# An interleaved attention and mixer kernel on one core: other planner constants, three mixer weight slots, later output projections

## The chip, the cores and the metric

The kernel runs on one NeuronCore of one Trainium2 chip. The metric is the device time of one execution in microseconds (us). Several runs of the same program are taken and the median is quoted. The profile is one further execution, recorded by the hardware profiler.

## What is computed

Four layers follow each other on a sequence of 2048 tokens of width 640: attention, mixer, attention, mixer (the same weights twice).

```
x = x + A(layernorm(x));  x = x + B(layernorm(x));  x = x + A(layernorm(x));  x = x + B(layernorm(x))
A: for each segment s of 32 tokens:  h = concat(mem, x_s)            # 8 + 32 rows
     q, k, v = h@Wq, h@Wk, h@Wv      # 32 heads of 192
     p = softmax(mask(q k^T * scale));  o = (p v) @ Wo;  mem = o[:8];  output o[8:]
B: h = gelu(layernorm(x)@w1); shift four column groups of h by +1, -1, +2, -2 tokens
   x1 = x + shifted(h)@w2;  out = x1 + gelu(layernorm(x1)@w3)@w4      # w3: 640 x 1536
```

The attention is a recurrence: segment s+1 needs the first 8 output rows of segment s. So a segment's output projection must be finished before the next segment's projections begin.

## The kernel before, in words

**Steps and lanes.** The attention runs in 69 steps (`T_A`). In a step lane 0 handles segment t of the first attention layer and lane 1 segment t-5 of the second one, side by side as 80 columns (2 x 40). The first five steps and the last five have one lane, 40 columns. A step works through 8 groups of 4 heads, two groups to a pair (`proj_pair`, `attend`, lines 479 to 629). For a pair, k, q and v are projected (line 495: 30 matmuls for a group and kind, each with its own 128x128 weight load). Then come, for each group, the scores `pss` (L559), mask and row minimum on VectorE (L570), exp on ScalarE (L577), the row sums on VectorE (L581 to L583), the transposed weights `pst` (L591), their copy `PT` (L596), `pso` (L605), its copy `oT` (L611) and the output projection into `psy` (L622, 30 matmuls against the resident `wo`). At the step's end ScalarE copies the memory rows of `psy` into the next step's `hT` (L640) and VectorE the others into `yTB` (L652); the next step's first matmul waits for `hT`.

**Mixer.** Every two steps one chunk of 64 tokens of both lanes (128 rows) goes through the mixer (`chunk`, `chunk_end`): psx, psl (transposes back), layernorm, w1 into `psh` (L873), gelu, w2 into `hs` (L901), layernorm, w3 into `psh2` in two halves (L933), gelu (L703 to L717), w4 into `y2` (L956, named y in the profile), the stores (L974) and the next attention's input. These instructions stand between those of the attention.

**Weights.** Part of Wk, Wq, Wv and all of Wo stay in SBUF. The rest is loaded again in every step: per pair 3 loads for k, 3 for q and 2 for v, 384 KB each (L420, tile `wst`), into a ring of 7 slots (`RING_A`). The mixer's weights are loaded again for each chunk, into a ring of 2 slots (`RING_B`, L443 to L449, tile `wstB`): w1 and w2 in three pieces (2, 2 and 1 rows of 128), w3 in 2 x 3, w4 in 6. All these loads are issued by SyncE's queue, in one order. A load waits there until the last matmul that reads its slot is done, and what is queued behind it waits too.

**The order of the work** is set before the launch by a planner (`Plan`, lines 66 to 217). Each operation has an engine, a duration, a due time and the buffers that it reads and writes. The planner simulates the engines and always places the operation that can start first, and among those that start at nearly the same time the one due earliest. What it places is then written out in that order on each engine. Its constants: `LAT` and `PE_LAT` are the handover from one engine to another, `DMA_RATE`, `DMA_LAT` and 0.8 us model a load (0.8 us, then the bytes at 380 GB/s one load after another, then 1.2 us).

**Homes.** PSUM has 8 banks: one for `psy` (class "y"), five for the attention's other tiles (class "A"), two for the mixer (class "B"). `oT` has 5 buffers. `xres` (bf16) holds the mixer's residual input, `xw` (f32) the sum, `gl` (f32) the gelu's intermediate, `PT` has two buffers.

Of the kernel before, what the change touches and what calls it, by code (L numbers as in the profile page):

```python
# [61 lines left out]
class Op:  # L62
    __slots__ = ("e", "d", "due", "fn", "n", "succ", "ready", "slots", "start", "end", "dma", "i")


class Plan:
# [8 lines left out]
    def add(self, e, d, due, fn, r=(), w=(), a=(), dma=0, queue=None):  # L75
        op = Op()
        op.e, op.d, op.due, op.fn, op.dma = e, d, due, fn, dma
# [34 lines left out]
    def place(self):  # L112
# [40 lines left out]
        while left:  # L153
# [67 lines left out]
def kernel(  # L221
# [107 lines left out]
    sm = [ctile([P, 16], f32, f"sm{i}") for i in range(4)]  # L329
# [15 lines left out]
    st4 = [ctile([P, 24], f32, f"st{i}") for i in range(4)]  # L345
# [11 lines left out]
    ALIAS = {("vx",): ("vb",), ("xo",): ("vb",), ("vx2",): ("uw",)}  # L357
# [26 lines left out]
    def mm_us(n, m=128, k=1):  # L384
        return k * (max(min(64, m), n) / 2400.0 + 0.0025)
# [44 lines left out]
    def load_b(nm, a, e, due, half=0):  # L430

        b = Slotted("rb", None)
        b.make = lambda: wring.tile([P, SLOT], bf16, name="wstB", tag=f"rb{b.slot}")
        n = e - a
        W = GW if nm == "w3" else Dm
# [4 lines left out]
        def fn(op):  # L440
            v = view()
            if nm == "w1":
                nc.sync.dma_start(out=v, in_=w1_v[:, a:e, :])  # L443
            elif nm == "w3":
                nc.sync.dma_start(out=v, in_=w3_v[:, a:e, GW * half:GW * (half + 1)])
# [4 lines left out]
        add("SP", DMA_ISSUE, due - LEAD_B, fn, w=(b,), dma=P * n * W * 2, queue="wb")  # L450
# [14 lines left out]
    def attention_step(t):  # L465
# [9 lines left out]
        psy = ps("y", [P, KC, NS], f32, "psy")  # L475
# [3 lines left out]
        def proj_pair(pr):  # L479
            s0 = base + sl * 2 * pr  # L480
            for kind, off in (("k", 0.0), ("q", 0.2), ("v", 0.5)):
                wbs, wv = load_pair(kind, pr, s0 + off * 2 * sl, LEAD_A)
                for j in range(2):
# [37 lines left out]
                    else:  # L521
# [12 lines left out]
                        for hf in range(2):  # L534
                            def fe(op, pvt=pvt, V_=V_, hf=hf):
                                src = T(pvt)[0:N, GWH * hf:GWH * (hf + 1)].rearrange("n (a b) -> n a b", a=2)
                                if hf:
                                    nc.vector.tensor_copy(out=v_runs(V_, hf)[0:N], in_=src)  # L538
                                else:
                                    nc.scalar.copy(out=v_runs(V_, hf)[0:N], in_=src)  # L540
# [3 lines left out]
        def v_runs(V_, hf):  # L544

            return V_[:, 512 * hf:512 * hf + 640].rearrange("n (a b) -> n a b", a=2)[:, :, 0:Dh]

        def attend(g):
# [31 lines left out]
            def f3(op):  # L580
                nc.vector.tensor_reduce(out=sm_[0:N, 4:4 + HG], in_=Pb[0:N, :, 0:N], axis=AX.X, op=ALU.add)  # L581
                nc.vector.reciprocal(out=sm_[0:N, 8:8 + HG], in_=sm_[0:N, 4:4 + HG])
                nc.vector.tensor_tensor(out=Pb[0:N, :, 0:N], in0=Pb[0:N, :, 0:N],  # L583
                                        in1=sm_[0:N, 8:8 + HG].unsqueeze(2).to_broadcast([N, HG, N]), op=ALU.mult)
# [8 lines left out]
            Pt = PT[G % 2]  # L593
# [3 lines left out]
            add("ACT", act_us(HG * N), hi - 4, f5, r=(pst,), w=(B("PT", G % 2),))  # L597
            pso = ps("A", [P, GC, NS], f32, "pso")

            def f6(op):  # L600
                o = T(pso)
                for hf in range(2):
                    for i2, col, c, st, sp in ((0, 0, 0, True, True), (0, 128, 1, True, False), (1, 256, 1, False, True),
                                               (1, 384, 2, True, True)):
                        nc.tensor.matmul(out=o[:, 3 * hf + c, 0:N], lhsT=V_[0:N, 512 * hf + col:512 * hf + col + P],  # L605
                                         rhs=Pt[0:N, 2 * hf + i2, 0:N], start=st, stop=sp)
            add("PE", mm_us(N, k=8), hi - 3, f6, r=(B("PT", G % 2), B("V", G % 2, 0), B("V", G % 2, 1)), w=(pso,))
# [118 lines left out]
    def chunk_loads(c):  # L726
# [22 lines left out]
        if edge:  # L749
            def fz(op):  # L750
                nc.gpsimd.memset(xres[:], 0.0)
                nc.gpsimd.memset(lnx[0:4, :], 0.0)
            add("POOL", 1.0, base, fz, w=(B("xres"), B("lnx", "l")))
        for lane, a, b, w0 in todo:
# [4 lines left out]
        for lane, k0 in look:  # L759
# [5 lines left out]
        if s < NSEG:  # L765
# [8 lines left out]
    def chunk(c):  # L774
# [65 lines left out]
        if c + 1 < NCH:  # L840
            chunk_loads(c + 1)
# [81 lines left out]
        for half in range(2):  # L923
            pz2 = [ps("B", [P, 3, XB], f32, "psh2") for _ in range(2)]
            for i, (a, e) in enumerate(((0, 2), (2, 4), (4, KC))):
                due = D(0.75 + 0.3 * half + 0.05 * i)
                wb, wv = load_b("w3", a, e, due, half)

                def fw(op, a=a, e=e, wv=wv, pz2=pz2):
                    w = wv()  # L930
                    for kc in range(a, e):
                        for n in range(6):
# [3 lines left out]
                add("PE", mm_us(128, k=6 * (e - a)), due, fw, r=(wb, vTk), a=tuple(pz2))  # L936
            for i in range(2):
# [134 lines left out]
```

## Time and profile before

| | us |
|---|---|
| median of 3 runs (lowest, highest) | 3990.78 (3970.34, 3994.87) |
| the profiled execution: its time, its span | 3971.5, 3969.8 |
| TensorE busy (share of the span) | 3493.2 (88%) |
| VectorE, ScalarE, GpSimd busy | 2608.1 (66%), 1550.0 (39%), 257.6 (6%) |
| DMA moved, mean rate | 1107.57 MB, 279 GB/s |
| the 59 steps with two lanes (292 to 3622) | 3330 |

The span goes from the first to the last instruction. Busy time is the sum of an engine's instructions; the ends of matmuls are modelled, so a run of n matmuls shows a little more than n times the pace of one. "Idle before" and the waits name the instruction or transfer that came last before an engine went on. PE is TensorE, DVE VectorE, ACT ScalarE, POOL GpSimd, SP SyncE. The names in the profile leave out buffer numbers, so psv is both the attention's v and a mixer tile.

### The profile page before, as it was taken

To read this page: it belongs to the slowest core of one execution; us is meant where nothing else is said; L and a number is where in the kernel's file an instruction comes from. 1 tells how busy PE (TensorE), PEld (TensorE's weight loads), DVE (VectorE), ACT (ScalarE), POOL (GpSimd) and SP (SyncE) were. 2 spreads that over 40 slices of the span, in tenths; PEclk is the share of its full clock that TensorE was granted. 3 is DMA by queue.
4 is the path that set the end of the run, shared out by engine and by line. 5 is a ranking of instruction groups with operands and counts; after the bars stand their busy time and mean duration, and the time that the engine had idled before them with its cause. 6 is when DMAs were issued, how large, how long until landed. Compare 5 with 4: busy or idle time off the path is not lost.

```text
span 3969.8 us, 187915 instructions
## 1 busy us (share of the span) xinstructions
PE 3493.2 (88%) x84703; PEld 3320.3 (84%) x84703; DVE 2608.1 (66%) x7611; ACT 1550.0 (39%) x3516; POOL 257.6 (6%) x467
## 2 busy tenths in 40 slices
PE   6888999999898988899998998898989999889884
PEld 5878888888888888888888888888888888888772
DVE  2566666667676666676666666676666676766562
ACT  1334434444343444344444444444344444433331
POOL 0000000000000000000000000000000000000000
PEclk6999999999999999999999999999999999999995
DMA  9888777888787888788888888788878888778883
GB/s 367 290 309 292 268 273 273 292 276 281 270 301 271 275 279 283 268 276 281 287 281 277 285 276 290 262 280 277 276 272 282 281 297 274 271 271 313 312 281 90
DMA packets 489637, 1107.57 MB, mean 279 GB/s; under 512 B 50302, under 2 KB 200076, under 8 KB 488832
## 3 DMA queue, kind: packets, MB, share of 16 engines
q1 hardware_dynamic: 481600, 1082.42, 79.1%
q8 instruction: 662, 10.85, 1.1%
q0 software_dynamic: 7232, 13.13, 1.0%
q14 instruction: 143, 1.17, 0.1%
HBM read 1090.10 MB, written 5.24 MB: 276 GB/s over the span
## 4 chain that ended last, share of the span: by engine, by line
PE 59%; DMA 34%; issue 2%; ACT 2%; DVE 2%; SPq 0%; POOL 0%; POOLq 0%; ACTq 0%; DVEq 0%
DMA wstB<-in_B_w_dram 21%; PE psy L622 12%; PE psk L495 11%; PE psv L495 10%; PE psq L495 8%; DMA wst<-in_A_Wq_dram 7%; PE pvt L532 3%; DMA wst<-in_A_Wk_dram 3%; PE pss L559 3%; PE y L956 3%; PE pso L605 3%; PE psh L933 2%; PE pst L591 2%; DMA wst<-in_A_Wv_dram 1%; PE hs L901 1%
## 5 line engine op out<-in xcount | busy, mean ns | idle before, releaser
L495 PEld LDWEIGHTS <-wst 128*128 128x128 bf16 x26496 | 1076.6, 100 | 94.8 <-DMA wst<-in_A_Wq_dram 37.9
L622 PE MATMUL psy<-oT,wo 128*128 128x80 bf16 (+1 forms) x16560 | 713.5, 201 | 34.1 <-issue 14.2
L622 PEld LDWEIGHTS <-wo 128*128 128x128 bf16 x16560 | 647.2, 101 | 51.9 <-issue 31.7
L505 ACT CAST qT<-psq 128x480 bf16<-128x480 f32 (+1 forms) x552 | 291.8, 530 | 921.6 <-PE psq L495 921.1
L570 DVE CUSTOM_DVE_ANT_1 pss<-pss,mask 80x320 f32<-80x320 f32 (+1 forms) x512 | 246.0, 480 | 487.0 <-PE pss L559 429.3
L495 PE MATMUL psq<-hT,wst 128*128 128x80 bf16 (+1 forms) x9936 | 472.0, 200 | 35.2 <-DMA wst<-in_A_Wq_dram 30.3
L495 PE MATMUL psk<-hT,wst 128*128 128x80 bf16 (+1 forms) x9936 | 468.4, 199 | 27.6 <-DMA wst<-in_A_Wk_dram 22.2
L611 DVE CAST oT<-pso 128x480 bf16<-128x480 f32 (+1 forms) x552 | 341.9, 619 | 183.9 <-PE pso L605 179.7
L495 PE MATMUL psv<-hT,wv 128*128 128x80 bf16 (+1 forms) x9936 | 442.9, 201 | 11.2 <-DMA wv<-in_A_Wv_dram 6.6
L525 ACT CAST vF<-psv 128x480 bf16<-128x480 f32 (+1 forms) x552 | 291.4, 528 | 286.5 <-PE psv L495 281.3
L495 PEld LDWEIGHTS <-wv 128*128 128x128 bf16 x9936 | 391.7, 101 | 12.9 <-DMA wv<-in_A_Wv_dram 7.3
L540 ACT COPY V<-pvt 80x384 bf16<-80x384 bf16 (+1 forms) x552 | 262.4, 475 | 304.3 <-PE pvt L532 255.7
L495 PE MATMUL psk<-hT,wk 128*128 128x80 bf16 (+1 forms) x6624 | 320.6, 199 | 45.8 <-ACT hT L640 40.0
L495 PE MATMUL psv<-hT,wst 128*128 128x80 bf16 (+1 forms) x6624 | 352.1, 201 | 7.0 <-DMA wst<-in_A_Wv_dram 6.2
L538 DVE COPY V<-pvt 80x384 bf16<-80x384 bf16 (+1 forms) x552 | 190.2, 349 | 242.9 <-ACT V L540 163.0
L519 DVE CAST kT<-psk 64x160 bf16<-64x160 f32 (+1 forms) x1104 | 336.8, 305 | 8.2
L577 ACT ACTIVATE Pm<-pss,sm 80x320 bf16<-80x320 f32 (+1 forms) x552 | 278.4, 505 | 141.4 <-DVE sm L570 138.9
L495 PE MATMUL psq<-hT,wq 128*128 128x80 bf16 (+1 forms) x6624 | 320.3, 199 | 3.7 <-DMA wq<-in_A_Wq_dram 3.3
L513 DVE CAST kT<-psk 128x320 bf16<-128x320 f32 (+1 forms) x552 | 255.4, 463 | 93.6 <-PE psk L495 83.8
L495 PEld LDWEIGHTS <-wk 128*128 128x128 bf16 x6624 | 270.4, 100 | 54.1 <-issue 53.5
L532 PE MATMUL pvt<-ident,vF 128*80 128x128 bf16 (+1 forms) x3312 | 286.7, 224 | 2.7 <-issue 1.2
L596 ACT COPY PT<-pst 80x320 bf16<-80x320 bf16 (+1 forms) x552 | 222.5, 403 | 170.0 <-PE pst L591 167.6
(108 smaller groups left out, 4603.0 us busy)
## 6 DMA issues: line engine op xcount, KB each, us to landing
wst<-in_A_Wk_dram SPq DMA_DIRECT2D x828, 384.0 KB, 5.1
wst<-in_A_Wq_dram SPq DMA_DIRECT2D x828, 384.0 KB, 5.9
wst<-in_A_Wv_dram SPq DMA_DIRECT2D x552, 384.0 KB, 4.8
wstB<-in_B_w_dram SPq DMA_DIRECT2D x350, 320.0 KB, 5.4
wstB<-in_B_w_dram SPq DMA_DIRECT2D x140, 384.0 KB, 5.5
wstB<-in_B_w_dram SPq DMA_DIRECT2D x70, 192.0 KB, 5.2
wstB<-in_B_w_dram SPq DMA_DIRECT2D x70, 160.0 KB, 4.5
wo<-in_A_Wo_dram SPq DMA_DIRECT2D x8, 960.0 KB, 12.3
```

The source lines that it names most:

```text
L495: nc.tensor.matmul(out=o[:, cc, 0:N], lhsT=wv(kc, GW * j + cc * P, GW * j + (cc + 1) * P), rhs=h[:, kc, c0:c0 + N], start=(kc == 0 and cc ...
L505: nc.scalar.copy(out=q[:, :, 0:N], in_=T(pq)[:, :, 0:N])
L513: nc.vector.tensor_copy(out=k4[:, :, 0::3, 0:N], in_=p4[:, :, 0::2, 0:N])
L519: nc.vector.tensor_copy(out=k4[r0:r1, :, jj, 0:N], in_=p4[r0:r1, :, 1, 0:N])
L525: nc.scalar.copy(out=vf[:, :, 0:N], in_=T(pq)[:, :, 0:N])
L532: nc.tensor.transpose(out=o[0:N, c * P:(c + 1) * P], in_=vf[:, c, 0:N], identity=ident[:, :])
L540: nc.scalar.copy(out=v_runs(V_, hf)[0:N], in_=src)
L570: nc.vector.tensor_tensor_reduce(out=o, in0=o, in1=maskt.unsqueeze(1).to_broadcast([N, HG, N]), scale=-scale, scalar=3.0e38, op0=ALU.add, ...
L577: nc.scalar.activation(out=Pb[0:N, :, 0:N], in_=o, func=ACT.Exp, bias=sm_[0:N, 0:1], scale=-1.0)
L596: nc.scalar.copy(out=Pt[0:N, :, 0:N], in_=T(pst)[0:N, :, 0:N])
L611: nc.vector.tensor_copy(out=o_[:, :, 0:N], in_=T(pso)[:, :, 0:N])
L622: nc.tensor.matmul(out=o[:, m, c0:c0 + N], lhsT=wo[:, cc, m * P:(m + 1) * P], rhs=o_[:, cc, 0:N], start=st, stop=True, skip_group_check=True)
```

## The change

- The planner's constants: `LAT` 0.2 to 0.1, `PE_LAT` 0.25 to 0.23; a load is now 0.8 us (`DMA_FIRST`), the bytes at 350 GB/s, then 2.6 us (`DMA_LAST`), and 0.6 us more for the mixer's loads (`B_MARGIN`). A 384 KB load takes 4.5 us in its model in place of 3.0. A matmul is planned at 54 columns at least.
- `RING_B` is 3; a slot is 1280 columns in place of 1536. So w3 is split in thirds of 5, 5 and 2 column blocks (loads 2, 2, 1 / 2, 2, 1 / one of all five rows), with 2, 2 and 1 gelus.
- `OT_BUFS` is 8. The rule at line 613 then gives groups 1 to 7 a due time at the step's end; group 0 keeps its earlier one. `psy` has no bank of its own: class "A" has 6.
- To make room in SBUF: `xw` is bf16 and shares its home with `xres`, `uw` is bf16, `gl` shares with `vb`, `PT` has one buffer, the `V` tile is regrouped. Since `xres` and `xw` are one tile, its loads for the next chunk are issued in `chunk_end`, behind the stores.

```diff
-RING_B = 2
+RING_B = 3
-PSUM_POOLS = {"y": 1, "A": 5, "B": 2}
-OT_BUFS = 5
-LAT = 0.2
-PE_LAT = 0.25
-DMA_RATE = 380.0e3
+Y_POOL = "A"
+PSUM_POOLS = {"A": 6, "B": 2}
+OT_BUFS = 8
+LAT = 0.1
+PE_LAT = 0.23
+DMA_RATE = 350.0e3
-DMA_LAT = 2.0
+DMA_FIRST = 0.8
+DMA_LAST = 2.6
+B_MARGIN = 0.6
...
-                srv = max(s + 0.8, srv) + o.dma / DMA_RATE
-                done = srv + DMA_LAT - 0.8
+                srv = max(s + DMA_FIRST, srv) + o.dma / DMA_RATE
+                done = srv + DMA_LAST + o.margin
...
-    Vt = [ctile([NS, 1152], bf16, f"V{i}") for i in range(2)]
+    Vt = [ctile([NS, HG, 256], bf16, f"V{i}") for i in range(2)]
-    PT = [ctile([NS, HG, NS], bf16, f"PT{i}") for i in range(2)]
+    PT = ctile([NS, HG, NS], bf16, "PT")
-    xres = ctile([XB, Dm], bf16, "xres")
-    xw = ctile([XB, Dm], f32, "xw")
+    xw = ctile([XB, Dm], bf16, "xw")
+    xres = xw
-    uw = h2u[:, 0:2 * Dm].bitcast(f32)
+    uw = h2u[:, 0:Dm]
-    vb = ctile([XB, Dm], bf16, "vb")
+    vbg = ctile([P, 6 * XB], bf16, "vbg")
+    vb = vbg[:, 0:Dm]
+    gl = vbg[:].bitcast(f32)
-    gl = ctile([P, 3 * XB], f32, "gl")
...
-        return k * (max(min(64, m), n) / 2400.0 + 0.0025)
+        return k * (max(54, n) / 2400.0 + 0.0025)
...
-        psy = ps("y", [P, KC, NS], f32, "psy")
+        psy = ps(Y_POOL, [P, KC, NS], f32, "psy")
...
-        for half in range(2):
-            pz2 = [ps("B", [P, 3, XB], f32, "psh2") for _ in range(2)]
-            for i, (a, e) in enumerate(((0, 2), (2, 4), (4, KC))):
-                due = D(0.75 + 0.3 * half + 0.05 * i)
-                wb, wv = load_b("w3", a, e, due, half)
+        for third, (n0, n1, units) in enumerate(((0, 5, ((0, 2), (2, 4), (4, KC))), (5, 10, ((0, 2), (2, 4), (4, KC))),
+                                                 (10, FC, ((0, KC),)))):
+            nb = (n1 - n0 + 2) // 3
+            pz2 = [ps("B", [P, 3, XB], f32, "psh2") for _ in range(nb)]
+            d0 = 0.75 + 0.25 * third
+            for i, (a, e) in enumerate(units):
+                due = D(d0 + 0.05 * i)
+                wb, wv = load_b("w3", a, e, due, n0 * P, n1 * P)
...
+        if c + 1 < NCH:
+            chunk_loads(c + 1, "x")
```

What the planner makes of it is shown at three places, in the middle of the run, where the order repeats every two steps. The first is SyncE's queue before, where the third piece of w1 and the pieces of w2 stand (`wst` are the attention's loads, `wstB` the mixer's, one row is one load).

```order
L420 DMA wst_49345<-in_A_Wk_dram 128x1536
L420 DMA wst_49348<-in_A_Wk_dram 128x1536
L443 DMA wstB_49433<-in_B_w1_dram 128x640
L449 DMA wstB_49442<-in_B_w2_dram 128x2x640
L449 DMA wstB_49520<-in_B_w2_dram 128x2x640
L420 DMA wst_49530<-in_A_Wk_dram 128x1536
```

In SyncE's queue of the changed kernel the three pieces of w1 stand together, here:

```order
L447 DMA wstB_48511<-in_B_w1_dram 128x2x640
L447 DMA wstB_48519<-in_B_w1_dram 128x2x640
L424 DMA wst_48537<-in_A_Wq_dram 128x1536
L447 DMA wstB_48554<-in_B_w1_dram 128x640
L424 DMA wst_48577<-in_A_Wv_dram 128x1536
L424 DMA wst_48618<-in_A_Wv_dram 128x1536
L424 DMA wst_48643<-in_A_Wk_dram 128x1536
```

Before, 21 loads of the attention stand between the second piece of w1 and the third, and w2 follows at once. Now one load stands between them, and 21 between the third piece and w2.

The second place is the same queue where the last piece of w2 and the first pieces of w3 stand, before:

```order
L420 DMA wst_49814<-in_A_Wk_dram 128x1536
L420 DMA wst_49822<-in_A_Wk_dram 128x1536
L449 DMA wstB_49834<-in_B_w2_dram 128x640
L445 DMA wstB_49855<-in_B_w3_dram 128x2x768
L420 DMA wst_49905<-in_A_Wk_dram 128x1536
```

and in the changed kernel, the three pieces of w2:

```order
L424 DMA wst_49566<-in_A_Wk_dram 128x1536
L453 DMA wstB_49581<-in_B_w2_dram 128x2x640
L453 DMA wstB_49600<-in_B_w2_dram 128x2x640
L453 DMA wstB_49655<-in_B_w2_dram 128x640
L424 DMA wst_49684<-in_A_Wq_dram 128x1536
```

The last piece of w2 now stands right behind the other two, in place of eight attention loads behind them.

The third place is TensorE at the end of a step, before (the last output projection, then the next step's k):

```order
L622 LDWEIGHTS wo_7_168
L622 MATMUL psy_49444<-oT3_121,wo_7_168 128x80
L495 LDWEIGHTS wk_0_149
L495 MATMUL psk_50568<-hT1_104,wk_0_149 128x80
L495 LDWEIGHTS wk_0_149
```

and in the changed kernel at the same step's end (after these rows ten mixer matmuls in all stand before the k projection):

```order
L625 LDWEIGHTS wo_7_168
L625 MATMUL psy_49583<-oT7_124,wo_7_168 128x80
L940 LDWEIGHTS wstB_50256
L940 MATMUL psh2_50681<-vT_135,wstB_50256 128x128
L940 LDWEIGHTS wstB_50256
```

A piece of w3 has moved between the last output projection and the next step's first k matmul, at every second step's end; at the others nothing stands between them, as before. Within the step the output projections have moved: before, those of groups 0 to 3 stand with the next pairs' projections and those of groups 4 to 7 behind the last v; now group 0 and 1 stand early and groups 2 to 7 at the end.

## Rows read from the trace of the kernel before

**Rows 1.** The page: busy shares, then the queue of all weight loads.

```profile
PE 3493.2 (88%) x84703; PEld 3320.3 (84%) x84703; DVE 2608.1 (66%) x7611; ACT 1550.0 (39%) x3516; POOL 257.6 (6%) x467
...
q1 hardware_dynamic: 481600, 1082.42, 79.1%
```

**Rows 2.** Windows: stretch, length, busy by engine, then PEclk, DMA share, GB/s.

```profile
292.00:3622.00 3330.00, 3001.93 (x72366) 2895.10 (x72363) 2284.97 (x6476) 1367.54 (x3004) 213.84 (x377) 0.99 0.81 279
...
1823.00:1828.00 5.00, 5.00 (x136) 5.00 (x134) 4.33 (x16) 2.89 (x7) 1.84 (x3) 1.00 1.02 364
1873.00:1878.00 5.00, 3.81 (x102) 3.60 (x100) 3.28 (x9) 0.75 (x2) 0.00 (x0) 1.00 0.06 19
```

**Rows 3.** Waits of TensorE, 292 to 3622: us in total, times, longest.

```profile
PE psh L933 <- DMA wstB<-in_B_w_dram: 69.4, 51, 3.9
PE psh L873 <- DMA wstB<-in_B_w_dram: 55.3, 29, 3.1
PE y L956 <- DMA wstB<-in_B_w_dram: 45.9, 34, 2.9
PE hs L901 <- DMA wstB<-in_B_w_dram: 39.8, 29, 2.2
PE psk L495 <- ACT hT L640: 37.0, 57, 1.0
PE psq L495 <- DMA wst<-in_A_Wq_dram: 21.8, 35, 1.3
PE psk L495 <- DMA wst<-in_A_Wk_dram: 15.9, 27, 1.6
```

**Rows 4.** Timeline of TensorE: start, length, instructions [idle before and its releaser].

```profile
1818.87 0.59 PE L495 MATMUL psk<-hT,wk 128*128 128x80 bf16 x12 [0.31 <-ACT hT L640]
...
1829.15 0.39 PE L495 MATMUL psk<-hT,wst 128*128 128x80 bf16 x6 [0.64 <-DMA wst<-in_A_Wk_dram]
...
1829.80 0.81 PE L495 MATMUL psk<-hT,wst 128*128 128x80 bf16 x18
...
1836.95 0.45 PE L873 MATMUL psh<-vT,wstB 128*128 128x128 bf16 x5 [1.14 <-DMA wstB<-in_B_w_dram]
...
1852.76 0.43 PE L901 MATMUL hs<-wstB,hTB 128*128 128x320 bf16 x2 [1.86 <-DMA wstB<-in_B_w_dram]
...
1866.34 0.51 PE L933 MATMUL psh<-vT,wstB 128*128 128x128 bf16 x6 [1.51 <-DMA wstB<-in_B_w_dram]
...
1875.93 0.59 PE L495 MATMUL psk<-hT,wk 128*128 128x80 bf16 x12 [0.98 <-ACT hT L640]
...
1878.07 0.84 PE L933 MATMUL psh<-vT,wstB 128*128 128x128 bf16 x12
```

**Rows 5.** The chain that ended last, pieces on loads: start, us, load waited for.

```profile
1823.68 5.42 DMA wst<-in_A_Wk_dram
...
1833.12 3.79 DMA wstB<-in_B_w_dram
...
1893.88 6.46 DMA wstB<-in_B_w_dram
```

**Rows 6.** Line L640 (ScalarE's copy of hT): its idle time until this releaser.

```profile
  DVE yTB L652: 16.3, 28
```

**Rows 7.** Groups by line: the copy PT (busy, mean ns, idle before).

```profile
L596 ACT COPY PT<-pst 80x320 bf16<-80x320 bf16 (+1 forms) x552 | 222.5, 403 | 170.0 <-PE pst L591 167.6
```

**Rows 8.** DMA issues: count, KB each, median us to landing.

```profile
xres<-x2d POOLq DMA_DIRECT2D x31, 80.0 KB, 5.5
```

**Rows 9.** Waits of TensorE behind the last full step, 3826 to 3970.

```profile
PE psh L933 <- DVE h2u L717: 8.3, 4, 2.6
PE y L956 <- DMA wstB<-in_B_w_dram: 8.1, 8, 1.8
```

**Rows 10.** Waits of TensorE in four one-lane steps, 93 to 292.

```profile
PE psv L495 <- DMA wst<-in_A_Wv_dram: 3.3, 3, 1.6
...
PE psq L495 <- DMA wst<-in_A_Wq_dram: 3.1, 6, 1.0
```

More of the change, by code (lines that the diff above doesn't have):

```diff
@@ L62 @@
 class Op:
-    __slots__ = ("e", "d", "due", "fn", "n", "succ", "ready", "slots", "start", "end", "dma", "i")
+    __slots__ = ("e", "d", "due", "fn", "n", "succ", "ready", "slots", "start", "end", "dma", "i", "margin")
 class Plan:
@@ L343 @@
     hTB = ctile([P, KC, TOK + 4, 2], bf16, "hTB")
-    gl = ctile([P, 3 * XB], f32, "gl")
-    st4 = [ctile([P, 24], f32, f"st{i}") for i in range(4)]
+    st4 = [ctile([P, 18], f32, f"st{i}") for i in range(4)]
     for i in range(2):
@@ L428, in load_pair, with load_b @@
         return (rb, *slots), view
-    def load_b(nm, a, e, due, half=0):
+    def load_b(nm, a, e, due, c0=0, c1=None):
         b = Slotted("rb", None)
-        b.make = lambda: wring.tile([P, SLOT], bf16, name="wstB", tag=f"rb{b.slot}")
+        b.make = lambda: wring.tile([P, 2 * Dm], bf16, name="wstB", tag=f"rb{b.slot}")
         n = e - a
-        W = GW if nm == "w3" else Dm
+        W = c1 - c0 if nm == "w3" else Dm
         def view():
@@ L449, in fn @@
                 nc.sync.dma_start(out=v, in_=w2_v[:, a:e, :])
-        add("SP", DMA_ISSUE, due - LEAD_B, fn, w=(b,), dma=P * n * W * 2, queue="wb")
+        add("SP", DMA_ISSUE, due - LEAD_B, fn, w=(b,), dma=P * n * W * 2, queue="wb",
+            margin=B_MARGIN)
         return b, view
@@ L602, in f6 @@
                 for hf in range(2):
-                    for i2, col, c, st, sp in ((0, 0, 0, True, True), (0, 128, 1, True, False), (1, 256, 1, False, True),
-                                               (1, 384, 2, True, True)):
-                        nc.tensor.matmul(out=o[:, 3 * hf + c, 0:N], lhsT=V_[0:N, 512 * hf + col:512 * hf + col + P],
+                    for i2, col, c, st, sp in ((0, 0, 0, True, True), (0, 128, 1, True, False), (1, 192, 1, False, True),
+                                               (1, 320, 2, True, True)):
+                        nc.tensor.matmul(out=o[:, 3 * hf + c, 0:N], lhsT=Vf[0:N, 512 * hf + col:512 * hf + col + P],
                                          rhs=Pt[0:N, 2 * hf + i2, 0:N], start=st, stop=sp)
-            add("PE", mm_us(N, k=8), hi - 3, f6, r=(B("PT", G % 2), B("V", G % 2, 0), B("V", G % 2, 1)), w=(pso,))
+            add("PE", mm_us(N, k=8), hi - 3, f6, r=(B("PT"), B("V", G % 2, 0), B("V", G % 2, 1)), w=(pso,))
             o_ = oT[G % OT_BUFS]
@@ L750, in fz @@
             def fz(op):
[L751 to L754, printed above, removed]
+                nc.gpsimd.memset(xres[:] if part == "x" else lnx[0:4, :], 0.0)
+            add("POOL", 1.0, base, fz, w=(B("xres") if part == "x" else B("lnx", "l"),))
+        if part == "x":
+            base = base + 0.6 * STEP
+        for lane, a, b, w0 in todo if part == "x" else ():
             def f(op, lane=lane, a=a, b=b, w0=w0):
@@ L758, in chunk_loads @@
             add("POOL", 0.9, base, f, r=rd, a=(B("xres"),), dma=(b - a) * Dm * 2)
-        for lane, k0 in look:
+        for lane, k0 in look if part == "l" else ():
             def f(op, lane=lane, k0=k0):
@@ L764, in chunk_loads @@
         s = 2 * c + 4
-        if s < NSEG:
+        if s < NSEG and part == "l":
             def f(op):
@@ L935, in fw @@
                                              skip_group_check=True)
-                add("PE", mm_us(128, k=6 * (e - a)), due, fw, r=(wb, vTk), a=tuple(pz2))
-            for i in range(2):
-                gelu(pz2[i], 3, D(0.9 + 0.3 * half + 0.05 * i),
-                     [(0, P, 0, 3, h2T[:, 6 * half + 3 * i:6 * half + 3 * i + 3, :])], (B("h2T", 2 * half + i),), (uk,))
+                add("PE", mm_us(128, k=(n1 - n0) * (e - a)), due, fw, r=(wb, vTk), a=tuple(pz2))
+            for i in range(nb):
+                m0, m1 = n0 + 3 * i, min(n0 + 3 * i + 3, n1)
+                gelu(pz2[i], m1 - m0, D(d0 + 0.12 + 0.05 * i), [(0, P, 0, m1 - m0, h2T[:, m0:m1, :])],
+                     (B("h2T", third, i),), (uk,))
     def chunk_end(c):
@@ L957, in fw @@
                                          start=(n == 0), stop=(n == FC - 1))
-            add("PE", mm_us(HC, k=2 * (e - a)), due, fw, r=(wb, B("uw"), *(B("h2T", k) for k in range(4))), a=tuple(y2))
+            add("PE", mm_us(HC, k=2 * (e - a)), due, fw, r=(wb, B("uw"), *(B("h2T", i, j) for i in range(3) for j in range(2) if i < 2 or j == 0)), a=tuple(y2))
         for k in range(2):
```

39 lines of the change are left out of this document (20 added, 19 removed).

## The prediction

> **What bounds the kernel now.** I read the page first: TensorE is busy for 88% of the span, VectorE for 66%, ScalarE for 39% [rows 1]. So TensorE's work, plus what TensorE waits for, makes the time. The queue with all weight loads is at 79.1% of the 16 engines' span [rows 1], so the transfers are not far behind.
>
> Then the windows: the 59 two-lane steps take 3330 us of the 3970, with a granted clock of 0.99 (2.4 GHz) [rows 2]. That is 56.4 us a step, or 112.9 us for two steps, which is one round of the order (a mixer chunk falls on two steps). TensorE is busy for 3001.9 us of these 3330, so some 328 us are idle, 11 us in two steps.
>
> Then the waits of that stretch: the four largest are all for the mixer's weights, 69.4 + 55.3 + 45.9 + 39.8 = 210.4 us in 143 waits. The attention's weights follow with 21.8 + 15.9 = 37.7 us in 62 waits, and hT at the steps' ends with 37.0 us in 57 [rows 3].
>
> A wait costs a little more than its idle time. A run of 6 matmuls shows 0.39 us, a run of 18 0.81 us [rows 4], so one matmul of 80 columns goes at 0.42/12 = 0.035 us, and a run has 0.39 - 0.21 = 0.18 us of its own, 0.15 us more than the pace. I add 0.15 us for each wait. A mixer matmul of 128 columns goes at (0.84 - 0.51)/6 = 0.055 us [rows 4].
>
> **Why TensorE waits for the mixer's weights.** A load can go out when the last matmul on its slot is done, and it is needed at its first matmul. In the order I count what TensorE does between the two, at these paces, and call it the cover. The wait is the time from the slot's release to the landing, less the cover. For w1's third piece there stand 10 mixer matmuls (0.55), 30 output projections (1.05), 18 of q (0.63) and 12 of pst and pso (0.4) between, a cover of 2.7 us; TensorE waited 1.14 us [rows 4], so the landing came 3.8 us behind the release, and the chain shows 3.79 for this load [rows 5]. For w2's third piece the cover is 3.8 and the wait 1.86 [rows 4], a landing after 5.7 us; for w3's third piece 4.05 and 1.51 [rows 4], 5.6 us. The method fits an attention load too: cover 4.9, wait 0.64 [rows 4], 5.5 us against 5.42 in the chain [rows 5]. So loads land 3.8 us after release with little in front of them, and otherwise after 5.4 to 6.5 [rows 5].
>
> **The change, part by part.**
>
> *Third mixer slot, and a planner that counts a load at 4.5 us and more.* By the same count in the new order, the 19 mixer loads of two steps have a cover of 8.5 us at least, most of them 9 to 16. That is over the 6.46 us of the longest piece [rows 5]. I see no mixer load in SyncE's queue in front of an attention load whose slot comes free earlier, so the third slot doesn't block the others. All 143 waits would go: 210.4 + 143 x 0.15 = 232 us. I leave 20 us for loads that meet a busy stretch, so minus 212. Bounds: minus 232, and nothing.
>
> *The attention's loads.* Their ring stays at 7 slots, and the plan moves them little: of 64 loads in two steps 7 have a cover under 6 us (4.6, 4.9, 5.3, 5.3, 5.5, 5.6, 5.9), where before 9 did. The first two are first loads behind a step's end, when the DMA engines have been idle (share 0.06 [rows 2]). Before, a load in that place had a cover of 4.3 us and no wait, so I count the other five. What changes is the load on the engines. Two steps carry 279 x 112.9 = 31.5 MB; at share 0.81 [rows 2] the full rate is 279/0.81 = 344 GB/s, so the transfers need 92 us of engine time in any two steps. Without the mixer's waits two steps take some 106 us, and the share goes from 0.81 to 0.86. At a step's end TensorE does only output projections, and no slot comes free. That stretch grows a little, from 7.6 to 8.2 us, and the rest of the step must take the loads at nearly the full rate (364 GB/s [rows 2]). So landings get later. I take 6.0 us in place of 5.5: the five loads then wait 0.7 + 0.7 + 0.5 + 0.4 + 0.1 = 2.4 us, with five restarts 3.2 us in two steps, or 94 us in 29.5 rounds. Now they cost 37.7 + 62 x 0.15 = 47. So plus 47. Bounds: minus 47 (landing as now, with nothing waiting) and plus 127 at 6.5 us. The nearest row is of the four one-lane steps, where 3.3 and 3.1 us are the two largest of these waits [rows 10]: 1.6 us a step, so 3.2 us in two steps, the value that I take.
>
> *Output projections at the step's end, hT.* Before, 28 of the 68 copies of hT came behind VectorE's copy of the same bank (16.3 us [rows 6]), and TensorE then waited 0.98 us, at the other ends 0.31 [rows 4]. In the new program the hT copy stands first at every end, and at every second end ten mixer matmuls (0.55 us) stand behind the last projection, which cover 0.31. There remain 29 waits of 0.31, 9 us of the 37.0 [rows 3]; I take minus 25. The tail of the last two groups (softmax, pst, pso, oT) has as much work between its links as before. Bounds: minus 37 and nothing. psy now takes one of six banks, from group 0's projection a quarter of the way into the step; so five are left for the other tiles, as before: nothing.
>
> *Single PT buffer.* The second PT copy must wait for the first pso. Between the two pso stands 1.07 us of TensorE work at least, the copy takes 0.40 [rows 7]: nothing, or up to 0.1 us for each of 552 if that cover were gone, 55 us.
>
> *Residual loads at the chunk's end.* Four DMA issues of GpSimd (two stores, two loads) now follow each other. Behind them on GpSimd stands only the copy of yTB's last columns and the next chunk's layernorm. From w4's last matmul to the next psx are 20 us of TensorE work; the landing takes 5.5 [rows 8]. Nothing; were it late, VectorE would stall in front of the mask of the scores, by a few us in 34 chunks.
>
> *w3 in thirds, bf16 residual, shared homes.* A gelu more in each chunk lies on ScalarE and VectorE, which have the room. In the tail, where nothing lies beside it, a round of gelus stops TensorE twice for 2.1 us (8.3 in 4 [rows 9]); two chunks make plus 8. Against it stand the tail's waits for the mixer's weights, 8.1 us in the largest row [rows 9]. Together nothing, 10 us either way. The bf16 sums are no slower than f32 ones.
>
> The sum, on the profiled execution: 3971.5 - 212 + 47 - 25 = 3781.5. I say 3780. The median of the runs lies 19 us above that execution, within their own spread of 25, and I add nothing for it. A measurement of this kernel can tell about 1% from no change.
>
> **The rivals.**
>
> *The transfers become the bound.* One more 384 KB load in front takes 1.08 us of the engines at 364 GB/s [rows 2], so landings go from 5.5 to 6.6 us. Then the five loads wait 5.4 us, the two first loads 0.3, with restarts 6.8 us in two steps, 200 us in all: 3971.5 - 237 - 47 + 200 = 3887. For it: 92 us of engine time in some 106, with two holes at the steps' ends in which the ring is full. Against it: now, at 0.81, the landings are already at 5.5 with bunched mixer loads in front, and the new queue spreads them.
>
> *Slower: the attention's ring is too short.* All loads go through one queue; TensorE, no longer held up by the mixer's loads, outruns the 7 slots, and the waits move from mixer to attention loads, which are twice as many. With landings at 7.2 us the five wait 8.4, four others some 2, restarts 1.3: 11.7 us in two steps, 346 us: 3971.5 - 284 + 346 = 4033. It decides from a landing of 7.0 us, where these waits reach some 9.6 us in two steps and take up all gains. Against it: a longer round also thins the load, and no row shows 7. The Trainium skill speaks for it: by "DMA: Bandwidth & Descriptors" (Latency and other measured facts) an access to HBM takes 0.2 us on average and 2 us at high load, which would add up to 1.8 us to a landing. The trace agrees in kind: 3.8 us with little in front, 5.4 to 6.5 in a full stretch [rows 5], though the queue in front would explain that too. By the rule the landing would be 5.5 + 1.8 = 7.3 us, this rival's time.
>
> *The mixer's waits stay.* If landings of mixer loads grow with the third slot, since each then has two more of its kind in front, TensorE waits as before, and only hT's 25 us go: 3946. It would take landings of over 8.5 us.
>
> *Better than forecast.* Attention waits as now and all mixer waits gone: 3971.5 - 232 - 28 = 3711, or 3665 without any attention wait.
>
> **How the numbers follow.** The forecast has 0.64 (3700 to 3840), the transfers as bound 0.17 (3840 to 3930), better 0.06, mixer's waits staying 0.06, slower 0.07. The range reaches from 3690 to 3890: it leaves out the last two, some of the better case and the far part of the second. Faster by over 1%: 0.64 + 0.06 + 0.16 = 0.86; within 1%: 0.07; slower 0.07.
>
> **What would show it.** Right: in two-lane steps the waits for wstB fall from 210 us to under 40; those for wst lie between 40 and 130; hT under 15; two steps take 105 to 107 us; DMA share about 0.86. Wrong: waits for wst over 200 us (the ring), wstB still over 100 (the slot), or a new row on PT, psy or gl over 30 us. If the wait rows fall as said and the time doesn't, TensorE's own pace has changed and the reading of the rows was wrong.

## The result, and the profile after

| | us |
|---|---|
| before, median of 4 runs (lowest, highest) | 3989.95 (3970.34, 3994.87) |
| after, median of 4 runs (lowest, highest) | 3741.58 (3739.40, 3755.23) |
| ratio, with its 95% interval | 0.939 [0.936, 0.943] |
| the profiled execution of after, its span | 3755.23, 3753.2 |

The changed kernel takes 248 us less, by 6.1%. The profiled execution of after is the slowest of its four, 14 us above the median.

First the page of after, which answers to [rows 1] (the columns are the same).

```profile
PE 3440.7 (92%) x84703; PEld 3285.7 (88%) x84703; DVE 2591.1 (69%) x7716; ACT 1531.9 (41%) x3586; POOL 246.1 (7%) x467
...
q1 hardware_dynamic: 504560, 1082.42, 81.5%
q8 instruction: 662, 10.85, 1.1%
```

TensorE does the same instructions and is now busy for 92% of the span. The last row is one to keep for later: a DMA queue of its own carries 662 packets with 10.85 MB of instructions.

Next the windows of after: the start and the one-lane steps, the two-lane steps, the last one-lane steps, and what stands behind the last step. They answer to [rows 2].

```profile
0.00:296.00 296.00, 230.82 (x6019) 205.16 (x6020) 138.19 (x521) 83.02 (x246) 16.89 (x43) 0.95 0.90 321
296.00:3409.00 3113.00, 2948.27 (x72340) 2854.52 (x72339) 2275.04 (x6565) 1352.14 (x3064) 204.52 (x379) 1.00 0.85 299
3409.00:3623.00 214.00, 185.26 (x4908) 164.27 (x4908) 119.93 (x444) 68.66 (x203) 15.28 (x27) 0.89 0.84 293
3623.00:3753.00 130.00, 76.39 (x1440) 61.79 (x1439) 57.92 (x188) 28.13 (x74) 9.38 (x18) 0.72 0.49 158
```

The two-lane steps take 3113 us in place of 3330, which is 105.5 us for two steps. TensorE is busy for 2948 us of them and idle for 165, where it was idle for 328. The DMA engines are at 0.85 of their time, where they were at 0.81 [rows 2].

Last TensorE's waits in those steps (waited for: us in total, times, longest), against [rows 3].

```profile
PE psv L500 <- issue: 43.3, 43, 2.0
PE psy L625 <- issue: 35.5, 46, 1.9
PE psq L500 <- issue: 20.3, 28, 1.6
PE psq L500 <- DMA wst<-in_A_Wq_dram: 9.6, 12, 1.8
PE psk L500 <- ACT hT L643: 9.1, 29, 0.3
...
PE psy L625 <- DVE oT L614: 6.1, 29, 0.2
...
PE psk L500 <- DMA wst<-in_A_Wk_dram: 3.8, 9, 0.9
```

The four rows for the mixer's weights are gone. hT is left with 29 waits of 0.31 us. The attention's weights, which were to cost more, cost less. The head of the list is new: waits that end with nothing that the profile shows ("issue").

For the comparison of all kernels I summed TensorE's idle times of 0.15 us and more by what ended them, from the fifth copy of hT to the 64th, which is where the steps have two lanes. Number of waits in brackets, us otherwise:

| kernel | two-lane steps | mixer's weights | attention's weights | hT | issue | engines | behind the last hT |
|---|---|---|---|---|---|---|---|
| before | 3329.6 | 210.4 (143) | 39.3 (65) | 37.0 (57) | 24.0 (42) | 8.9 | 143.4 |
| after | 3113.2 | 0 | 15.1 (26) | 9.1 (29) | 121.8 (147) | 14.7 | 130.4 |
| before_new_times | 3147.7 | 5.7 (11) | 16.8 (37) | 36.9 (58) | 69.2 (109) | 44.3 | 153.1 |
| two_slots | 3077.3 | 2.5 (3) | 14.6 (31) | 19.7 (59) | 73.3 (113) | 9.5 | 156.8 |
| old_times | 3157.7 | 32.1 (32) | 98.4 (146) | 9.1 (29) | 59.2 (86) | 3.2 | 129.9 |
| two_slots_old_times | 3330.3 | 154.6 (132) | 131.6 (159) | 19.6 (59) | 19.1 (29) | 7.7 | 157.6 |
| half_bytes | 2933.8 | 0 | 0 | 9.1 (29) | 0 | 14.0 | 120.9 |
| five_held | 3155.4 | 0 | 9.4 (22) | 9.1 (29) | 101.1 (145) | 67.0 | 132.0 |
| late_third | 3099.8 | 2.3 (4) | 9.5 (24) | 19.8 (59) | 87.6 (124) | 9.8 | 130.6 |
| ring_a6 | 3128.9 | 0 | 27.0 (51) | 9.9 (30) | 98.0 (131) | 25.4 | 129.3 |

So the span went from 3969.8 to 3753.2, 216.6 us. The two-lane steps give 216.4, the end behind the last hT gives 13.0, and the one-lane steps take 12.7 back (3.2 ahead of the two-lane steps and 9.5 behind them). Within the two-lane steps the waits of the table fall from 319.6 to 160.7, by 158.9, and TensorE's busy time falls by 53.7 (from 3001.9 [rows 2] to 2948.3).

### The profile page after: what moved, and what is told of

It is laid out like the page before. It is cut to its first block, busy times and chain, and to the rows that moved or that the text cites. A ratio compares the mean times of both kernels' runs of the same rounds, so it can differ in the third digit from the quotient of the medians.

```text
span 3753.2 us, 188743 instructions
## 1 busy us (share of the span) xinstructions
PE 3440.7 (92%) x84703; PEld 3285.7 (88%) x84703; DVE 2591.1 (69%) x7716; ACT 1531.9 (41%) x3586; POOL 246.1 (7%) x467
## 3 DMA queue, kind: packets, MB, share of 16 engines
q8 instruction: 662, 10.85, 1.1%
## 5 line engine op out<-in xcount | busy, mean ns | idle before, releaser
L500 PEld LDWEIGHTS <-wst 128*128 128x128 bf16 x26496 | 1089.6, 100 | 100.8 <-issue 54.9
L625 PE MATMUL psy<-oT,wo 128*128 128x80 bf16 (+1 forms) x16560 | 690.4, 200 | 58.8 <-issue 39.9
L625 PEld LDWEIGHTS <-wo 128*128 128x128 bf16 x16560 | 624.2, 100 | 73.0 <-issue 61.9
L510 ACT CAST qT<-psq 128x480 bf16<-128x480 f32 (+1 forms) x552 | 284.1, 530 | 855.3 <-PE psq L500 851.6
L500 PE MATMUL psq<-hT,wst 128*128 128x80 bf16 (+1 forms) x9936 | 485.8, 199 | 35.3 <-issue 20.9
L500 PE MATMUL psk<-hT,wst 128*128 128x80 bf16 (+1 forms) x9936 | 478.3, 200 | 14.3 <-issue 8.8
L500 PE MATMUL psv<-hT,wv 128*128 128x80 bf16 (+1 forms) x9936 | 432.5, 199 | 31.2 <-issue 30.6
L500 PEld LDWEIGHTS <-wv 128*128 128x128 bf16 x9936 | 381.8, 100 | 37.7 <-issue 33.6
L537 PE MATMUL pvt<-ident,vF 128*80 128x128 bf16 (+1 forms) x3312 | 286.1, 223 | 12.7 <-ACT vF L530 5.2
L583 DVE TENSOR_REDUCE sm<-Pm 80x4 f32<-80x320 bf16 (+1 forms) x552 | 250.2, 453 | 67.2 <-ACT Pm L579 55.5
L500 PEld LDWEIGHTS <-wq 128*128 128x128 bf16 x6624 | 269.4, 100 | 24.8 <-issue 10.3
```

Of the source, the lines that this page charges most:

```text
L500: nc.tensor.matmul(out=o[:, cc, 0:N], lhsT=wv(kc, GW * j + cc * P, GW * j + (cc + 1) * P), rhs=h[:, kc, c0:c0 + N], start=(kc == 0 and cc ...
L510: nc.scalar.copy(out=q[:, :, 0:N], in_=T(pq)[:, :, 0:N])
L537: nc.tensor.transpose(out=o[0:N, c * P:(c + 1) * P], in_=vf[:, c, 0:N], identity=ident[:, :])
L583: nc.vector.tensor_reduce(out=sm_[0:N, 2:2 + HG], in_=Pb[0:N, :, 0:N], axis=AX.X, op=ALU.add)
L625: nc.tensor.matmul(out=o[:, m, c0:c0 + N], lhsT=wo[:, cc, m * P:(m + 1) * P], rhs=o_[:, cc, 0:N], start=st, stop=True, skip_group_check=True)
```

## The experiments

Two questions were put. Which part of the change takes the mixer's waits away: the planner's times (theory A) or the third slot (theory B)? And what are the waits by "issue" (theory C says: TensorE's instructions are themselves fetched over the DMA engines, and come late when these are full)? A' is the form that A and B took after the first runs: either of the two is enough.

**The times alone, in the kernel before** (e1_before_new_times):

```diff
-LAT = 0.2
-PE_LAT = 0.25
-DMA_RATE = 380.0e3
+LAT = 0.1
+PE_LAT = 0.23
+DMA_RATE = 350.0e3
...
-                srv = max(s + 0.8, srv) + o.dma / DMA_RATE
-                done = srv + DMA_LAT - 0.8
+                srv = max(s + DMA_FIRST, srv) + o.dma / DMA_RATE
+                done = srv + DMA_LAST + o.margin
```

with 0.8, 2.6 and a margin of 0.6 us for the mixer's loads, as in after.

> The kernel before with the planner's new times alone (two mixer slots, five held outputs, all homes as before). Theory A, the planner's times do the work: in this order the smallest cover of a mixer load is 5.6 us (2.7 before), that of an attention load 5.7 (4.3 before), so the waits for wstB in the two-lane steps fall from 210 us to under 40, those for wst to under 30, the waits called issue rise from 24 to 80 or more, and the time is 3730 to 3800. Rival B, the third slot does it: waits for wstB stay over 150 us, the time is over 3900.

Measured: 3817.03 us (3810.98 to 3823.09), 0.958 [0.955, 0.961] of before. TensorE's waits from 300 to 3448 in this kernel, same columns as above:

```profile
PE psy L625 <- DVE oT L614: 39.7, 88, 0.8
PE psk L498 <- ACT hT L643: 36.9, 58, 1.0
PE psy L625 <- issue: 24.4, 32, 1.8
...
PE psh L876 <- DMA wstB<-in_B_w_dram: 2.8, 3, 1.6
```

Two slots are enough for the mixer once the planner counts a load at its real length: 210.4 us of waits become 5.7. The waits by "issue" rose to 69.2 us, where 80 or more were expected. The time came out 17 us above the range and 75 us above after. Three differences from after are seen, and how they share the 75 us was not tried apart: hT stays at 36.9 us, as before; the waits for oT rise to 39.7 us, from 7.3 in before; and the end behind the last hT takes 153.1 us in place of 130.4.

**The change with two slots** (e2_two_slots), and **the change with the old times** (e3_old_times):

```diff
-RING_B = 3
+RING_B = 2
```

```diff
-LAT = 0.1
-PE_LAT = 0.23
-DMA_RATE = 350.0e3
+LAT = 0.2
+PE_LAT = 0.25
+DMA_RATE = 380.0e3
...
-DMA_LAST = 2.6
-B_MARGIN = 0.6
+DMA_LAST = 1.2
+B_MARGIN = 0.0
```

> The changed kernel with two mixer slots in place of three. Theory A: one mixer load in two steps has a cover of 4.2 us, one more under 6, so wstB costs some 40 us and the attention's loads some 40; the time is 3770 to 3840. Rival B (the slot does it): wstB over 120 us, the time over 3870.

> The changed kernel with the planner's old times (landing 3.0 us in its model, handover 0.2), three slots kept. Theory A: two mixer loads in two steps have a cover of 3.4 us and five attention loads one under 5, so wstB costs some 110 us, wst some 120, issue less than 60; the time is 3880 to 3970. Rival B (the slot does it): wstB under 40 us, the time within 1.5% of 3742.

Measured: 3761.24 us (3750.62 to 3772.88), 0.944 [0.941, 0.948], with two slots; 3797.63 us (3785.61 to 3805.93), 0.953 [0.949, 0.957], with the old times. TensorE's waits from 300 to 3400 with the old times:

```profile
PE psk L500 <- DMA wst<-in_A_Wk_dram: 58.5, 74, 1.7
PE psq L500 <- DMA wst<-in_A_Wq_dram: 31.4, 59, 2.0
PE y L964 <- DMA wstB<-in_B_w_dram: 30.8, 31, 2.7
```

Without the third slot the mixer's waits stay at 2.5 us and the attention's at 14.6, where some 40 each were expected; the two-lane steps are no longer than in after, and the time lies 9 us below the range. Without the new times the mixer's waits stay at 32.1, against my expectation by A that about 110 us of them would come back; waits and time are what rival B had named (under 40 us, within 1.5% of 3742). So neither part is needed for the mixer where the other is there. What the old times do bring is attention waits, 98.4 us: the old plan reckons a 384 KB load at 3.0 us, where the rows have over 5, and in its order five attention loads in two steps have a cover under 5 us.

**Both out** (e5_two_slots_old_times) is the test of that: with the two edits above together, and everything else of the change in place.

> The changed kernel with two mixer slots and the planner's old times: only the held outputs and the homes of the change are left. Theory A', the new times and the third slot are two ways to the same cover, either of which takes most of the mixer's waits away: without both, wstB is at 150 us or more in the two-lane steps, wst at 60 or more, issue under 40, and the time within 1.5% of the kernel before (3930 to 4050). Rival E, the held outputs and homes carry a good part of the gain: under 3900.

Measured: 3999.68 us (10 runs, 3967.38 to 4010.60), 1.003 [1.000, 1.006] of before. TensorE's waits from 297 to 3627:

```profile
PE psk L500 <- DMA wst<-in_A_Wk_dram: 67.9, 57, 3.3
PE hs L905 <- DMA wstB<-in_B_w_dram: 56.8, 29, 3.5
PE psh L877 <- DMA wstB<-in_B_w_dram: 46.6, 29, 2.7
PE y L964 <- DMA wstB<-in_B_w_dram: 37.3, 50, 2.0
```

All that the change gained is gone again, though held outputs, shared homes, w3 in thirds and the bf16 residual are still there. The waits for weights are 286 us, where before had 250. So the gain needs one of the two, and the rest of the change shows no gain of its own without them.

**Half of the bytes** (e4_half_bytes), for the waits by "issue". Each streamed load brings only the first half of its columns; the slots are zeroed tiles, and every matmul, its order and its instruction stay. This leaves out the products with half of the streamed weights.

```diff
+    ringA = [ctile([P, SLOT], bf16, f"wst{i}") for i in range(RING_A)]
+    ringB = [ctile([P, 2 * Dm], bf16, f"wstB{i}") for i in range(RING_B)]
...
-                nc.sync.dma_start(out=T(b)[:, 0:PW], in_=w_src[kind][:, kc, cols])
+                nc.sync.dma_start(out=T(b)[:, 0:GW], in_=w_src[kind][:, kc, PW * pr:PW * pr + GW])
...
-                nc.sync.dma_start(out=v, in_=w1_v[:, a:e, :])
+                nc.sync.dma_start(out=v[:, :, 0:320], in_=w1_v[:, a:e, 0:320])
```

> The changed kernel with the same order, in which every streamed weight load brings only the first half of its columns (the other half of each slot is zero, so half of the projections' and of the mixer's products are left out). Theory C, the new waits called issue are TensorE's instruction fetches that come late because the DMA engines are full: they fall from 121 us in the two-lane steps to under 20, the time to 3560 to 3650, with DMA share near 0.45. Rival D, a fetch has its own latency, whatever the load: issue stays over 90 us, and only the 15 us of wst waits go: 3700 to 3740.

Measured: 3507.59 us (3505.55 to 3508.68), 0.880 [0.878, 0.883]. Its DMA queues from 263 to 3197 (packets, MB, share of 16 engines):

```profile
q1 hardware_dynamic: 420891, 453.65, 52.7%
q8 instruction: 566, 9.27, 1.3%
```

and its waits there, from the top of the list:

```profile
PE psk L504 <- ACT hT L647: 9.4, 30, 0.3
PE psy L629 <- DVE oT L618: 6.1, 29, 0.2
```

The same 566 instruction packets are fetched, and no wait of 0.15 us by "issue" is left in the two-lane steps. So these waits do not come from TensorE's own issue, which is the same here and less held up than in after. They come with the load on the DMA engines, whose share is 0.55 here (near 0.45 was expected) and 0.85 in after. The time fell some 50 us below the expected range: the one-lane steps and the end got shorter too, by 67 us together. There, too, most of after's waits for weights and by "issue" are gone.

**Five held outputs and a bank for psy** (e6_five_held):

```diff
-Y_POOL = "A"
-PSUM_POOLS = {"A": 6, "B": 2}
-OT_BUFS = 8
+Y_POOL = "y"
+PSUM_POOLS = {"y": 1, "A": 5, "B": 2}
+OT_BUFS = 5
```

> The changed kernel with five oT buffers and a bank of its own for psy, so four groups' output projections stand earlier, as before. Theory A': the cover of the mixer's loads stays at 5.7 us and more, so the time is within 1% of 3742; the waits for oT rise from 6 us in the two-lane steps to some 30, issue falls a little. Rival F (the held outputs make the cover): wstB over 60 us, the time over 3800.

Measured: 3792.84 us (3786.71 to 3803.96), 0.951 [0.948, 0.954]: 51 us over after, more than I allowed. TensorE's waits from 298 to 3454:

```profile
PE psy L625 <- DVE oT L614: 30.6, 59, 1.0
...
PE pso L608 <- ACT PT L598: 16.7, 28, 0.6
PE pst L593 <- DVE Pm L585: 14.1, 37, 0.6
```

hT has the same 29 short waits as after, so its gain does not hang on the eight held outputs, as the prediction had it. What they (or the sixth bank, which goes with them here; the two were not tried apart) save is inside the step: 67.0 us of waits on other engines, mostly for oT, PT and Pm, in place of 14.7. A likely reason, not tried: with room to put the output projections off, the planner has other work to place between the links of a group's chain.

**A third slot only for the end** (e7_late_third). With two slots the two-lane steps were no longer, but the end behind the last hT was 157 us in place of 130, so I gave the slot out late:

```diff
     plan = Plan(classes)
+    plan.free_slots["rb"] = [(0.0, 0), (0.0, 1), (3250.0, 2)]
```

> The changed kernel, in which the third mixer slot is given out only at the end of the run (its order is that with two slots until there). If the third slot earns its time in the tail alone and costs instruction fetches in the two-lane steps, the two-lane steps take 3060 to 3095 us as with two slots (3113 with three), the part behind the last full step 125 to 135 as with three (157 with two), and the time is 3710 to 3740. Rival: the differences of the stretches between two and three slots are noise; then 3740 to 3765.

Measured: 3739.09 us (3719.88 to 3746.17), 0.937 [0.933, 0.940]. Waits for the mixer's weights and the gelu behind the last step, in two_slots first:

```profile
PE psh L940 <- DVE h2u L720: 14.1, 6, 2.7
PE y L964 <- DMA wstB<-in_B_w_dram: 8.5, 8, 2.0
```

and in late_third:

```profile
PE psh L941 <- DVE h2u L721: 9.9, 4, 2.8
...
PE y L965 <- DMA wstB<-in_B_w_dram: 3.4, 5, 1.0
```

The end is 130.6 us as in after. The two-lane steps, whose order on TensorE is that of two_slots up to there, took 3099.8 us against 3077.3 (3060 to 3095 were expected): so 22 us is what one profiled execution can differ from another in this stretch, and the 36 us between two_slots and after are not much more. The median can't be told from after's 3741.58 (the intervals of the ratios overlap). It is not shown to be the better kernel.

**Six slots for the attention** (e8_ring_a6): RING_A 7 to 6.

> The changed kernel with six attention slots in place of seven, so less is in flight in front of an instruction fetch. Theory C (fetches late behind queued loads): issue falls from 122 us in the two-lane steps to under 95; wst rises from 15 to 50 to 110, as 81 loads have a cover under 5 us; the time 3730 to 3830. Rival D' (a fetch is late because of the share of the engines, not of what is queued): issue within 15 us of 122.

Measured: 3773.23 us (3771.41 to 3782.95), 0.946 [0.944, 0.949]. That is within the expected range and 32 us above after. Attention waits rise to 27.0 us only, less than expected: with one slot fewer the ring still isn't short, and the rival of the prediction in which 7 slots are too few is far off. "Issue" falls to 98.0, between what theory C (under 95) and rival D' (107 and more) had named, and the 24 us are about as much as two executions differ by in that stretch. So the run doesn't decide between the two.

## Why the prediction was right

The forecast was 3780, the median is 3741.58; on the profiled execution it was 3781.5, and that execution took 3755.2. The mechanism was right. One term of the sum was wrong, the attention's loads, and two were missing, TensorE's late instructions and its clock. These errors went against each other, so that the sum comes closer than its terms is in part luck.

**Mixer's waits, minus 212.** They fell from 210.4 to nothing by their idle time alone; what the restarts add is in the busy time, below. The reason, a cover of 8.5 us and more against landings of 6.5, held where it counts: the 72 mixer loads of after's two-lane steps with a cover of 8.5 us or less land 5.2 us behind the release of their slot (median). That the cover comes from the third slot and the planner together was said; that either alone would do was not, and the runs show it: 5.7 us without the slot in the old kernel, 32.1 without the times.

**Attention's loads, plus 47.** This is the step that failed. I took one landing for all, 6.0 us in place of 5.5, and held it against the five covers of 5.3 to 5.9: waits of 3.2 us in two steps, 94 us in all. The waits fell to 15.1. The DMA share rose to 0.85 as said. From issue to landing (the median of each kind, DMA issues of after from 296 to 3409):

```profile
wst<-in_A_Wk_dram SPq DMA_DIRECT2D x708, 384.0 KB, 5.6
wst<-in_A_Wq_dram SPq DMA_DIRECT2D x708, 384.0 KB, 5.9
wst<-in_A_Wv_dram SPq DMA_DIRECT2D x472, 384.0 KB, 5.3
```

and the same rows of before from 292 to 3622:

```profile
wst<-in_A_Wk_dram SPq DMA_DIRECT2D x708, 384.0 KB, 5.0
wst<-in_A_Wq_dram SPq DMA_DIRECT2D x708, 384.0 KB, 5.9
wst<-in_A_Wv_dram SPq DMA_DIRECT2D x472, 384.0 KB, 4.7
```

Half a microsecond was added to the shorter ones, nothing to the longest. Counted from the release of the slot, as the prediction counts it, the median of all attention loads went from 5.5 to 5.9 us: for the ring as a whole the 6.0 was right. It was wrong for the loads that it was held against. With each load's slot and readers taken from the order and the times from the trace, the five shortest covers of a round next to the two first loads are 5.1 to 5.8 us in after, and these loads land after 4.6 to 5.5 (medians). They wait 10 times, 4.4 us in all, where five waits in each of 29.5 rounds and 71 us of idle time were forecast. In before two loads of a round with covers of 4.9 and 5.1 landed after 5.1 and 5.9, and made 43 of the 65 waits and 27.3 of their 39.3 us; the most that one load of the round makes in after is 8 waits with 6.7 us, at a cover of 6.1. Why the loads with a short cover land sooner is not shown.

So of the bounds minus 47 to plus 127 the truth lies near the lower end, minus 24 and the restarts. The nearest row that I had taken, the one-lane steps [rows 10], was no guide; the DMA share there is 0.88 (before, 93 to 292). The rival with 7.2 us, for which the Trainium skill's "DMA: Bandwidth & Descriptors" (Latency and other measured facts) spoke with an access of 2 us at high load, did not come: no median of the attention's loads rose by more than 0.6.

**hT, minus 25.** It fell by 27.9, to the 29 waits of 0.31 us that were counted in the order. In this trace:

```profile
1816.25 1.24 PE L625 MATMUL psy<-oT,wo 128*128 128x80 bf16 x30 [0.21 <-DVE oT L614]
1817.80 0.59 PE L500 MATMUL psk<-hT,wk 128*128 128x80 bf16 x12 [0.31 <-ACT hT L643]
...
1875.59 0.72 PE L940 MATMUL psh<-vT,wstB 128*128 128x128 bf16 x10
1876.15 0.59 PE L500 MATMUL psk<-hT,wk 128*128 128x80 bf16 x12
```

At one end TensorE waits 0.31 us, at the next ten mixer matmuls stand in between and it doesn't. VectorE's copy of the same bank now stands behind ScalarE's each time, so the waits of 0.98 us [rows 4] are gone:

```profile
L655 DVE CAST yTB<-psy 128x160 bf16<-128x160 f32 x128 | 37.9, 347 | 128.9 <-ACT hT L643 128.5 <-PE psy L625 0.4
```

The cause was put in the wrong place: five_held keeps the 9.1 us without the eight held outputs. In the changed kernel with two slots there are 59 waits with 19.7 us at the new times and 19.6 at the old; with three slots there are 29 with 9.1 at either. So the mixer matmuls at every second end come with the third slot. ScalarE's copy came late behind VectorE's 28 times in before and in before_new_times, 2 times in two_slots, 3 in two_slots_old_times, and never in after, old_times and five_held: the order of the copies comes with neither the new times nor the held outputs, but with something in the rest of the change, which was not tried apart.

**The edits at nothing.** The single PT buffer costs what was said. ScalarE waits for its release, and TensorE hardly ever for it (all of after, who waited for PT):

```profile
  ACT PT L598: 99.3, 133
  PE pso L608: 2.6, 7
```

The residual's loads were late once, for 3.3 us. The end was to cost 8 us more for the gelus and get 8 back; it got 13.0 shorter (143.4 to 130.4), mostly by the third slot: two_slots has 156.8 there. The shared bank at nothing was not tried by itself: five_held puts it and the eight held outputs together at some 50 us.

**What was not in the sum.** 97.8 us more of waits by "issue" (last section), and 53.7 us less of TensorE's busy time. Of the latter some 13 us are restarts: the waits of the table, those on engines with them, went from 341 to 251 in number, at the 0.15 us of the prediction. Most of the rest is the clock. Here is a wait for the mixer's weights in before, with the same output projections ahead of it and behind it (timeline of TensorE),

```profile
475.94 1.25 PE L622 MATMUL psy<-oT,wo 128*128 128x80 bf16 x30
...
480.01 0.45 PE L873 MATMUL psh<-vT,wstB 128*128 128x128 bf16 x5 [1.89 <-DMA wstB<-in_B_w_dram]
...
481.55 2.20 PE L622 MATMUL psy<-oT,wo 128*128 128x80 bf16 x30
```

and the granted clock in the second run of projections (windows of before; third number from the end):

```profile
481.00:484.00 3.00, 3.00 (x48) 3.00 (x46) 2.45 (x8) 1.39 (x3) 0.00 (x0) 0.50 0.81 259
```

A granted clock of 0.50 is 1.2 GHz. In before's two-lane steps TensorE has it for 99 us, in 28 stretches; 24 of them begin within 1.4 us of the end of a wait of 1.8 to 3.2 us for the mixer's weights. Not every such wait is followed by one. In after it is 11 us in 4 stretches. A matmul of 80 columns goes at 67 ns in these stretches and at 36 outside them (medians). An estimate from these numbers: before's 96 us of busy time at the lower clock would be 52 at the higher, after's 11 would be 6, so the clock gives some 39 of the 53.7 us. The prediction read the clock as 0.99 and priced a wait at its idle time and 0.15 us; the long waits cost this much more.

In figures, for the two-lane steps: the sum was minus 190 and they fell by 216. Mixer and hT gave the 238 that the idle times show, the attention's waits gave 24 where 47 were to be paid, busy time gave 54 (that is 316); late instructions took 98 back and waits between engines 6. The 4 us that are left over lie in gaps under 0.15 us.

## What to carry to other kernels

Where a planner sets the order, look first at the length that it gives a load against the trace's own (3.0 us in the plan, 5 to 6 in the rows here): that number, with the handover times that were changed beside it, was worth some 170 us in the old program, and a deeper ring hides the same error (old_times, two_slots_old_times). Count the cover, the engine's work between a slot's release and the next first use, and compare it with the landing; but take the landing from loads with a cover as short as those in question: one landing for all forecast 71 us of idle time here where 4 came. A wait can cost more than its idle time; look at the granted clock behind the long ones. When the waits for data are gone, look at what else goes over the DMA engines: a part of the gain goes to whatever comes late next.

## What the runs showed of the hardware

The instructions of TensorE come over the DMA engines. A run of projections on resident weights, which wait for no load, stops in its middle (timeline of TensorE in after):

```profile
1835.91 0.78 PE L500 MATMUL psv<-hT,wv 128*128 128x80 bf16 x17
1838.72 0.21 PE L500 MATMUL psv<-hT,wv 128*128 128x80 bf16 x1 [2.03 <-issue]
```

In that time the DMA engines are full (windows of after; the last two numbers are DMA share and GB/s, and a share of 1 or a little more means full),

```profile
1833.60:1836.60 3.00, 3.00 (x81) 2.95 (x78) 2.61 (x7) 1.92 (x6) 0.00 (x0) 1.00 0.95 341
1836.70:1838.70 2.00, 0.00 (x0) 0.00 (x0) 0.63 (x2) 0.39 (x1) 0.00 (x0) 1.00 1.06 385
```

and one packet of the instruction queue lies in it (DMA queues of after, 1836 to 1838):

```profile
q1 hardware_dynamic: 566, 0.75, 104.7%
q8 instruction: 1, 0.02, 2.8%
```

That packet ran from 1836.26 to 1837.17, and TensorE went on 1.55 us behind its end. Worked out over all 147 such waits of after's two-lane steps: TensorE goes on 1.39 us behind the end of an instruction packet (median; 1.24 to 1.59 for the middle 90%), where the other 104 waits end 0.43 to 5.1 us behind one (middle 90%). 662 packets of 10.85 MB are 16.4 KB each, and 2 x 84703 matmuls and weight loads over 662 packets make 256 instructions a packet. Counted in TensorE's own order, the 147 waits stand at whole multiples of 256 instructions from one another, one more or less, so each lies where one packet's instructions end and the next one's begin. The packet itself takes as long with half the bytes (0.98 us, median) as here (0.99), so it is its start that comes late. No trace shows the request. But matched with the blocks in order, a block's packet starts, in the median of 566, 2.3 us behind TensorE's first instruction of the block before it in after, 1.8 us in before and 0.5 us in half_bytes; a block takes 5.4 us in after. At the 147 waits it is 3.5 us, at after's other blocks 1.8. So the packet is fetched about one block ahead, and its later start under load uses up that lead.

The Trainium skill's "Runtime: NRT & Kernel Launch" (Instruction fetch mechanics) has blocks of 16 KiB and 256 instructions, as counted here, and calls the cost of crossing from one to the next mostly hidden. That holds for half_bytes, at a DMA share of 0.55, where none of 566 shows. It does not for after at 0.85: 147 of 566 show, and cost 121.8 us, 3.9% of the two-lane steps; at before's 0.81 it was 42 with 24.0 us. The share alone does not say how many: two_slots, at 0.86, has 113 with 73.3 us. How much is in flight at once may be what differs, with two slots in place of three; ring_a6, with one attention slot fewer at 0.85, has 131 with 98.0 us, which is too close to settle it. late_third, with TensorE's order of two_slots in these steps, has 124 with 87.6, so that some 11 waits and 14 us are chance.
